# Paced loads in the first three steps, constants and the first plan on GpSimd, and a later first weight load, in an attention and mixture-of-experts kernel

## The chip, the cores and the metric

The kernel runs on one core of a Trainium2 chip. The metric is device microseconds of one execution; lower is better. The kernel before takes 458.71 us in the median of three runs (458.58 to 460.1).

## The reference, cut to what matters

```python
# q, k, v: (4, 8, 768, 64); every position sees 8 global keys and the 96 last ones
scores = q @ k.T / 8 - slope[h] * dist;  scores = where(keep, scores, -1e9)
x = softmax(scores) @ v                       # regrouped to rows: (3072, 512)
logits = x @ w_gate + modality_bias[modality_id]
e_idx, gate_w = argmax(logits), softmax(logits)[e_idx]        # 8 experts, top 1
for e in range(8):
    m = e_idx == e
    out[m] = gate_w[m] * (relu(x[m] @ w1[e]) @ w2[e])         # 512 -> 1024 -> 512
```

## The kernel before, in words

**Attention** goes over 24 blocks of 128 rows (6 to each of the 4 batches), in a software pipeline that is written out by hand in `step(n)` (L1054), for n from 0 to 24. Step n does the score matmuls of block n (`s_mm`, L210, 32 of them), adds the bias and takes the maximum of its 8 heads on VectorE (`red`, L229) and their exponentials on ScalarE (L240); it transposes the probabilities of block n-1 (`t_mm`, L254; copied back by `t_cp`, L263 on VectorE and L261 on ScalarE), does the value matmuls of block n-2 (`pv`, L276 with the tile `vl`, then L288 with `vx`) and scales them into rows (`xr`, L309) that go to the HBM tensor `x_rows` (L316). The gate's small matmuls run three and four steps behind (`gate_a`, `gate_b`, `gate_c`).

**Loads.** All come from the one queue of SyncE (SP), in the order of its program: `qt` and `kt` of block n+2 and `vx`, `vl` of block n are issued in step n, with three buffers each, so a load waits only for the matmuls that last read its buffer. At the start `load_0` and the loads of block 1 come first, then those of step 0 without any wait. Steps 3 to 10 also write zeros to the table of sorted tokens (`consts_c`, L974).

**Work set for a step.** `at(n, f)` adds work to the end of step n. For batch b the routing is `route_a` (maximum, exponential, one-hot), `route_b` (counts by matmul, running base on GpSimd), `route_d` (two sums, a reciprocal, the place of each token, all on VectorE) and `route_c` (a GpSimd scatter of token ids for each block), in steps 9, 10, 11 and from 12 on for batch 0, and six steps later for batch 1. `consts_b` (L939 to L946) and `consts_d` (L953 to L961) make constants on VectorE in steps 3 and 4.

**The plan of the first units.** After batch 1 is routed, `plan_e` works out on VectorE, in four parts in steps 17, 18, 18 and 19, which expert and which rows the first three full units of 256 tokens have (`items`, L418, and `slots`, L488). SP reads the result into registers (`ld_w` L588, `ld_x` L570) and then loads the first unit's weights: `w1` of the expert in quarters in steps 19 and 20 (L598, 512 KB each), `w2` in step 22 (L600). `split` (L609 on ScalarE, L610 on VectorE) makes high and low parts of one quarter at the end of each of the steps 21 to 24.

**The expert layers** (14 units, L638 to L640 and L679 to L681) then run with TensorE always busy. The order on TensorE, VectorE and ScalarE is fixed as written (`manual_schedule`); the order on SP and GpSimd is the scheduler's own. Three lines show where the change hooks in: a wait can be put on any instruction with `spaced`, and `last` always holds the newest ScalarE instruction.

```python
def spaced(ins, by=last):                       # L106: ins waits for by[0]
last[0] = nc.scalar.activation(...)             # L240, in red
at(LAST - 1 + (0, 1, 1, 2)[j], plan_e)          # L1018, LAST = 18
```

Of the kernel before, what the change touches and what calls it, by code (L numbers as in the profile page):

```python
# [12 lines left out]
I32 = mybir.dt.int32  # L13
# [25 lines left out]
NE = 3  # L39
BE = 2  # L40
# [30 lines left out]
def moe_attention_kernel(  # L71
# [56 lines left out]
    def load_k(n):  # L128

        kts[n] = qkn.tile([P, NP, KW], F32, tag="kt", name=f"kt{n}")  # L130
        nc.sync.dma_start(kts[n], k_t[n])

    def load_v(n):

        vx = qkn.tile([P, 2, DM], F32, tag="vx", name=f"vx{n}", bufs=3)
        vl = qkn.tile([P, 2, NP, D], F32, tag="vl", name=f"vl{n}", bufs=3)
        vxs[n] = vx, vl
        nc.sync.dma_start(vx, v_l[n])
        for h in range(2):
            nc.sync.dma_start(vl[64 * h : 64 * h + SM], v_s[n, h])  # L140
# [208 lines left out]

    def route_a(b):  # L350
# [5 lines left out]
        ex = t3(b, "ex")  # L356
        nc.scalar.activation(ex, dl, AF.Exp)
# [6 lines left out]
        rt[b] = oh  # L364
        rt[b, "ex"] = ex
# [25 lines left out]
    def route_d(b):  # L391
        se = t2(b, "se")
        V.reduce_sum(se, rt.pop((b, "ex")), axis=AX.X)
        V.tensor_scalar_add(se, se, 1e-9)
        V.reciprocal(tki.bitcast(F32)[:, b * NB : (b + 1) * NB, 1], se)
        pf = t2(b, "pf")
        V.reduce_sum(pf, rt.pop((b, "pos")), axis=AX.X)
        pi = t2(b, "pi", I32)
        V.tensor_copy(pi, pf)
# [18 lines left out]
    def items(tag, pool, cnt, used, ni, first):  # L418
# [6 lines left out]
        left = cnt  # L425
        if used is not None:
            left = pl("left", [E])
            V.scalar_tensor_tensor(left, used, -float(U), cnt, ALU.mult, ALU.add)
# [11 lines left out]
        if first:  # L440

            V.tensor_scalar(first_used, cex, -1.0, float(first), ALU.mult, ALU.add)
            V.tensor_scalar(first_used, first_used, 0.0, None, ALU.max)
            V.tensor_tensor(first_used, first_used, full, ALU.min)
# [11 lines left out]
        if not first:  # L456
            rem = pl("rem", [E])
            V.scalar_tensor_tensor(rem, full, -float(U), left, ALU.mult, ALU.add)
            key = pl("key", [E])
            V.scalar_tensor_tensor(key, rem, 8.0, erev, ALU.mult, ALU.add)  # L460
            V.tensor_tensor(t88, bm(key, E), bc(key, E), ALU.is_gt)
            rr = pl("rr", [E])
            V.reduce_sum(rr, t88, axis=AX.X)
            V.tensor_scalar(rr, rr, cin[:, E - 1 : E], None, ALU.add)
            V.tensor_scalar(key, rem, 0.0, 1000.0, ALU.is_equal, ALU.mult)
            V.tensor_add(rr, rr, key)
            yield
            V.tensor_tensor(m2, bm(rr, ni), uc, ALU.is_equal)
            V.tensor_add(m1, m1, m2)
            V.tensor_tensor(m2, m2, bm(full, ni), ALU.mult)  # L470
            V.tensor_add(st, st, m2)
            if used is not None:
                V.tensor_tensor(m2, m1, bm(used, ni), ALU.mult)
                V.tensor_add(st, st, m2)
            yield
# [416 lines left out]
    uidx = const.tile([P, NLT], F32, name="uidx")  # L892
    le = const.tile([P, E, E], F32, name="le")
# [13 lines left out]
    def consts_a():  # L907
# [5 lines left out]
        nc.gpsimd.iota(uidx, pattern=[[1, NLT]], base=0, **ciota)  # L913
        nc.gpsimd.memset(tki, 0)
# [19 lines left out]
    def consts_b():  # L934
# [4 lines left out]
        V.tensor_copy(m1, mi[:, :, 0])  # L939
        V.tensor_scalar(m0, m1, -1.0, 1.0, ALU.mult, ALU.add)  # L940
        V.tensor_tensor(gsame, bc(uidx[:, 0:NGT], NR), bm(uidx[:, 0:NR], NGT), ALU.is_equal)
        tb1 = gp.tile([P, NBLK, E], F32, tag="tb1", name="tb1", bufs=1)
        V.tensor_tensor(tbias, bc(m0, E), bm(mb[:, 0, :], NBLK), ALU.mult)
        V.tensor_tensor(tb1, bc(m1, E), bm(mb[:, 1, :], NBLK), ALU.mult)
        V.tensor_add(tbias, tbias, tb1)
        V.tensor_tensor(le, bm(eidx, E), bc(eidx, E), ALU.is_le)  # L946

    def consts_d():
# [28 lines left out]
    for b in range(B):  # L977
        n0 = b * NB
        at(n0 + NB + 3, route_a, b)
        at(n0 + NB + 4, route_b, b)  # L980
        at(n0 + NB + 5, route_d, b)
# [10 lines left out]
    early = {}  # L992

    def run(name, g, f=None):

        try:
            next(g)
        except StopIteration as r:
            f(r.value)
            return False  # L1000
        return True


# [3 lines left out]
    def planned_e(r):  # L1007
        uei, uoi, inv = slots("e", plan, *r, NE, 2)
# [3 lines left out]
    def plan_e(g=[]):  # L1012
        if not g:
# [40 lines left out]
    def step(n):  # L1054

        on, back = n < NBLK, 0 < n <= NBLK
        if on:
            load_v(n)
# [286 lines left out]
```

## Time and profile before

| what | value |
|---|---|
| median of the runs | 458.71 us |
| the profiled execution, its own time | 461.01 us |
| its span, first to last instruction | 459.2 us |
| TensorE busy | 439.6 us (96%) |
| VectorE / ScalarE / GpSimd busy | 323.7 / 283.5 / 100.9 us |
| mean granted TensorE clock | 0.991 |

Times are microseconds from the start of the span. A busy time is summed over an engine's instructions; `[2.37 <-DMA kt<-in_k_t]` behind an instruction is the idle time of its engine just before it and what ended it. SPq rows are issues of transfers. A step is read here by the start of its 32 score matmuls (L210).

### The profile page before, as it was taken

The numbers are of one execution on the slowest core, as the hardware profiler recorded it, in microseconds if no ns is written. First come the engines' busy times: TensorE is split into PE (matmuls) and PEld (weight loads), VectorE is DVE, ScalarE is ACT, GpSimd is POOL, SyncE is SP. The second block draws the span as 40 slices with busy tenths as digits, with TensorE's granted clock in tenths as the row PEclk, the third lists the DMA queues.
The fourth block names the chain that finished last, engine by engine and source line by source line (L and its number), as shares of the span: only waits on it lengthen the run. The fifth ranks groups of instructions, "written<-read, shape, count | busy, mean of one in ns | idle before, by whom it ended". The sixth has DMA issues, their size and how long they took to land.

```text
span 459.2 us, 12892 instructions
## 1 busy us (share of the span) xinstructions
PE 439.6 (96%) x4828; PEld 387.6 (84%) x4828; DVE 323.7 (70%) x973; ACT 283.5 (62%) x687; POOL 100.9 (22%) x144
## 2 busy tenths in 40 slices
PE   5799999998988999999999999999999999999994
PEld 5688888887877798989898988989889898899993
DVE  4789888889988669896656596574965648667450
ACT  5678887887777554554545486454854557655541
POOL 7000002123306341631312112213122040300101
PEclk9799999999999999999999999999999999999999
DMA  7999999999799919576757679666796666965101
GB/s 231 327 343 337 347 334 332 324 323 310 257 297 330 340 50 328 187 237 226 264 215 245 213 255 362 215 226 226 242 380 238 210 229 208 360 244 185 46 2 51
DMA packets 42870, 115.69 MB, mean 252 GB/s; under 512 B 8943, under 2 KB 10991, under 8 KB 42800
## 3 DMA queue, kind: packets, MB, share of 16 engines
q1 hardware_dynamic: 38032, 101.74, 66.4%
q0 software_dynamic: 4768, 13.05, 7.5%
q8 instruction: 40, 0.66, 0.6%
q14 instruction: 30, 0.25, 0.2%
HBM read 100.40 MB, written 14.63 MB: 250 GB/s over the span
## 4 chain that ended last, share of the span: by engine, by line
PE 81%; DVE 7%; issue 6%; DMA 3%; ACT 2%; SPq 0%; POOL 0%; POOLq 0%; DVEq 0%; ACTq 0%
PE pt L254 7%; PE phs L638 6%; PE phs L640 6%; PE phs L639 6%; PE pos L681 6%; PE pos L680 6%; PE pos L679 6%; PE s L210 5%; PE x L288 4%; PE phe L638 2%; PE poe L679 2%; PE poe L681 2%; PE poe L680 2%; PE phe L640 2%; PE phe L639 2%
## 5 line engine op out<-in xcount | busy, mean ns | idle before, releaser
L240 ACT ACTIVATE pr<-sc,nmx 128x168 f32<-128x168 f32 x192 | 81.2, 425 | 26.1 <-DVE nmx L229 26.1
L640 PE MATMUL phs<-xhs,als 128*128 128x256 f32 x256 | 72.3, 282 | 0.0
L638 PE MATMUL phs<-xhs,ahs 128*128 128x256 f32 x256 | 72.2, 282 | 0.0
L639 PE MATMUL phs<-xls,ahs 128*128 128x256 f32 x256 | 72.1, 282 | 0.0
L645 DVE SCALAR_TENSOR_TENSOR hls<-phs,hhs 128x512 fp32r<-128x512 f32 x32 | 22.1, 692 | 51.8 <-ACT hhs L644 51.8
L229 DVE CUSTOM_DVE_ANT_0 sc<-s,tbl 128x168 f32<-128x168 f32 x192 | 50.7, 329 | 10.9 <-PE s L210 9.9
L254 PE MATMUL pt<-ident,pr 128*128 128x128 f32 x288 | 46.3, 292 | 5.4 <-DVE pT L263 3.0
L679 PE MATMUL pos<-bhs,hhs 128*128 128x512 f32 x128 | 51.4, 401 | 0.0
L681 PE MATMUL pos<-bhs,hls 128*128 128x512 f32 x128 | 50.6, 395 | 0.0
L680 PE MATMUL pos<-bls,hhs 128*128 128x512 f32 x128 | 50.5, 395 | 0.0
L644 ACT ACTIVATE hhs<-phs 128x512 fp32r<-128x512 f32 x32 | 19.1, 598 | 48.9 <-PE phs L640 48.9
L638 PEld LDWEIGHTS phs<-xhs,ahs 128*128 128x128 f32 x256 | 48.9, 191 | 0.4
L639 PEld LDWEIGHTS phs<-xls,ahs 128*128 128x128 f32 x256 | 48.8, 191 | 0.3
L640 PEld LDWEIGHTS phs<-xhs,als 128*128 128x128 f32 x256 | 48.8, 191 | 0.0
L577 POOL DMA_INDIRECT xgs<-x_rows,uis x16 | 20.9, 1304 | 126.6 <-DMA uis<-ids_sorted 63.8
L254 PEld LDWEIGHTS pt<-ident,pr 128*128 128x128 f32 x288 | 31.2, 144 | 17.8 <-DVE pT L263 8.9
L263 DVE COPY pT<-pt 128x384 f32<-128x384 f32 x72 | 37.2, 545 | 6.9 <-PE pt L254 6.8
L210 PE MATMUL s<-kt,qt 64*64 64x168 f32 x768 | 36.6, 321 | 3.9 <-DMA kt<-in_k_t 3.9
L405 POOL DMA_INDIRECT ids_sorted<-tki,pi x24 | 25.3, 1055 | 62.5 <-PE x L288 28.4
L240 ACT ACTIVATION_READ_ACCUMULATOR pr<-sc,nmx 128x1 f32 x192 | 36.3, 189 | 0.0
L210 PEld LDWEIGHTS s<-kt,qt 64*64 64x64 f32 x768 | 27.5, 138 | 6.9 <-issue 5.0
L697 POOL DMA_INDIRECT out<-obs,ois x16 | 17.4, 1089 | 54.2 <-ACT obs L696 52.0
(322 smaller groups left out, 1054.8 us busy)
## 6 DMA issues: line engine op xcount, KB each, us to landing
vx<-in_v_l SPq DMA_DIRECT2D x24, 512.0 KB, 6.5
kt<-in_k_t SPq DMA_DIRECT2D x23, 464.0 KB, 6.7
x_rows<-xr SPq DMA_DIRECT2D x24, 256.0 KB, 5.5
qt<-in_q_t SPq DMA_DIRECT2D x23, 256.0 KB, 5.3
vl<-in_v_s SPq DMA_DIRECT2D x48, 96.0 KB, 5.7
rawe0a<-in_moe_w SPq DMA_DIRECT2D x4, 512.0 KB, 4.9
rawe0b<-in_w SPq DMA_DIRECT2D x4, 512.0 KB, 6.5
rawe1a<-in_moe_w SPq DMA_DIRECT2D x4, 512.0 KB, 3.7
```

Of the source, the lines that this page charges most:

```text
L210: nc.tensor.matmul(ps[h][64 * half : 64 * half + 64, c : c + W], qt[hs, hp, 64 * half : 64 * half + 64], kt[hs, hp, k0 : k0 + W], start=Tr ...
L229: V.tensor_tensor_reduce(out=sc, in0=pss[n, hp // 2][h][:, hp % 2 * W : (hp % 2 + 1) * W], in1=(tbl0 if n % NB == 0 else tbl)[:, hh, :], o ...
L240: last[0] = nc.scalar.activation(pr[:, h * (PRW - W) : h * (PRW - W) + W], sc, AF.Exp, bias=nmx[:, hh : hh + 1], scale=-1.0, accum_out=sum ...
L254: nc.tensor.transpose(tp[:, j * P : (j + 1) * P], pr[:, o : o + P], ident)
L263: V.tensor_copy(pT.rearrange("p a b -> p (a b)"), tp[:, 0 : 3 * P])
L405: ins = nc.gpsimd.indirect_dma_start(out=ids, out_offset=bass.IndirectOffsetOnAxis(ap=pi[:, j : j + 1], axis=0), in_=tki[:, b * NB + j, :] ...
L638: nc.tensor.matmul(o, hi[:, fs], s.xh[:, c, :], start=(c == 0), stop=False)
L639: nc.tensor.matmul(o, hi[:, fs], s.xl[:, c, :], start=False, stop=False)
L640: nc.tensor.matmul(o, lo[:, fs], s.xh[:, c, :], start=False, stop=(c == 3))
L679: nc.tensor.matmul(s.po[t], s.hh[:, fc, tt], hi[:, wv], start=(fc == 0), stop=False)
L680: nc.tensor.matmul(s.po[t], s.hh[:, fc, tt], lo[:, wv], start=False, stop=False)
L681: nc.tensor.matmul(s.po[t], s.hl[:, fc, tt], hi[:, wv], start=False, stop=(fc == 7))
```

## The change

**The start.** A new `paced` puts a wait on the newest ScalarE instruction of the program before a load, for `qt` and `kt` of blocks 2 to 4 and for `vx` and `vl` of blocks 0 to 2. In steps 0 to 2 the loads of `qt` and `kt` are issued behind the first six heads of `red`, so they wait for the sixth exponential of the step; the value loads of block n-1 are issued at the start of step n (for n from 1 to 3) and wait for the last ScalarE instruction of step n-1. **GpSimd.** `consts_b`, `consts_d`, all of `plan_e` (one piece in step 17) and the two sums of `route_d` for batches 0 to 2 go to GpSimd; a sum over eight becomes three adds of halves (`folded`), a comparison a subtraction and a comparison with zero (`over`). The exponential of `route_a` becomes `route_e`, one step later. **Weights.** The quarters of the first unit's `w1` are loaded in steps 20 and 22, its `w2` in step 24.

```diff
+    def paced(ins, early):
+        if early:
+            spaced(ins)
     def load_q(n):
-        nc.sync.dma_start(qts[n], q_t[n])
+        paced(nc.sync.dma_start(qts[n], q_t[n]), 1 < n < NPACE + 2)     # NPACE = 3
     def load_v(n):
-        nc.sync.dma_start(vx, v_l[n])
+        paced(nc.sync.dma_start(vx, v_l[n]), n < NPACE)
...
+    def folded(r, t):
+        G = nc.gpsimd
+        h = E // 2
+        while h > 1:
+            G.tensor_add(t[:, :, 0:h], t[:, :, 0:h], t[:, :, h : 2 * h])
+            h //= 2
+        G.tensor_add(r.unsqueeze(2), t[:, :, 0:1], t[:, :, 1:2])
+    def over(r, a, b, op):
+        nc.gpsimd.tensor_tensor(r, a, b, ALU.subtract)
+        nc.gpsimd.tensor_scalar(r, r, 0.0, None, op)
...
+    def route_e(b):
+        ex = t3(b, "ex")
+        nc.scalar.activation(ex, rt.pop((b, "dl")), AF.Exp)
-    def route_d(b):
+    def route_d(b, eng):
         se = t2(b, "se")
-        V.reduce_sum(se, rt.pop((b, "ex")), axis=AX.X)
-        V.tensor_scalar_add(se, se, 1e-9)
+        pf = t2(b, "pf")
+        for r, t in ((se, rt.pop((b, "ex"))), (pf, rt.pop((b, "pos")))):
+            if eng is V:
+                V.reduce_sum(r, t, axis=AX.X)
+            else:
+                folded(r, t)
+        eng.tensor_scalar(se, se, 1e-9, None, ALU.add)
         V.reciprocal(tki.bitcast(F32)[:, b * NB : (b + 1) * NB, 1], se)
...
-        V.tensor_copy(m1, mi[:, :, 0])              # consts_b, consts_d: V -> nc.gpsimd
+        nc.gpsimd.tensor_copy(m1, mi[:, :, 0])
...
-    for j in range(4):
-        at(LAST - 1 + (0, 1, 1, 2)[j], plan_e)
+    at(LAST - 1, plan_e)                            # its sums by folded, on GpSimd
...
-    at(LAST + 1, lambda: ld_w(eslots[0], "a", (0, 1)))
-    at(LAST + 2, lambda: ld_w(eslots[0], "a", (2, 3)))
+    at(LAST + 2, lambda: ld_w(eslots[0], "a", (0, 1)))
+    at(LAST + 4, lambda: ld_w(eslots[0], "a", (2, 3)))
-    at(LAST + 4, lambda: ld_w(eslots[0], "b"))
+    at(LAST + 6, lambda: ld_w(eslots[0], "b"))
...
     def step(n):
-        if on:
+        if 0 < n <= NPACE:
+            load_v(n - 1)
+        if NPACE <= n < NBLK:
             load_v(n)
-        if n + 2 < NBLK:
+        if NPACE <= n < NBLK - 2:
             load_q(n + 2)
             load_k(n + 2)
...                                                 # behind red of six heads:
+        if n < NPACE:
+            load_q(n + 2)
+            load_k(n + 2)
```

**The order on SP at the start**, before, from the load of block 1 on (`qt1` is the tile qt of block 1):

```order
L118 DMA qt1_82<-in_q_t 128x512
L131 DMA kt1_84<-in_k_t 128x928
L138 DMA vx0_225<-in_v_l 128x1024
L140 DMA vl0_226<-in_v_s 48x512 x2
L118 DMA qt2_230<-in_q_t 128x512
L131 DMA kt2_232<-in_k_t 128x928
L138 DMA vx1_280<-in_v_l 128x1024
L140 DMA vl1_281<-in_v_s 48x512 x2
L928 DMA cst_182<-in_small 128x196
L118 DMA qt3_285<-in_q_t 128x512
L131 DMA kt3_287<-in_k_t 128x928
L138 DMA vx2_374<-in_v_l 128x1024
```

and of the change, from the wait for the sixth exponential of step 0 (on `qt2`) to the value loads of block 2:

```order
L124 DMA qt2_266<-in_q_t 128x512
L137 DMA kt2_268<-in_k_t 128x928
L144 DMA vx0_276<-in_v_l 128x1024
L146 DMA vl0_277<-in_v_s 48x512 x2
L124 DMA qt3_322<-in_q_t 128x512
L137 DMA kt3_324<-in_k_t 128x928
...
L124 DMA qt4_416<-in_q_t 128x512
L137 DMA kt4_418<-in_k_t 128x928
L124 DMA qt5_501<-in_q_t 128x512
L137 DMA kt5_503<-in_k_t 128x928
L322 DMA x_rows<-xr0_475 128x512
L144 DMA vx2_491<-in_v_l 128x1024
```

The value loads of block 0 have moved behind `qt`, `kt` of block 2, and those of block 2 behind `qt`, `kt` of blocks 4 and 5 and the first write of rows.

**The order on VectorE at the end of step 17**, before, from the last gate addition to the first reduction of step 18 (the nine L430 to L444 are the first part of the plan):

```order
L342 TENSOR_TENSOR lgt_2486<-lq_1_2641,tbias 128x8
L393 TENSOR_REDUCE se_2645<-ex_2344 128x6
L394 TENSOR_SCALAR se_2645<-se_2645 128x6
L395 RECIPROCAL tki<-se_2645 128x6
L397 TENSOR_REDUCE pf_2649<-pos_2503 128x6
L399 CAST pi_2651<-pf_2649 128x6
L430 CAST cie<-base 128x8
...
L444 TENSOR_TENSOR first_used<-first_used,fulle 128x8
L229 ISA sc_0_2698,nmx_2697<-s_0_0_2676,tbl_130 128x168
```

and of the change:

```order
L269 COPY pT_2_2643<-pt_2_2639 128x384
L348 TENSOR_TENSOR lgt_2494<-lq_1_2651,tbias 128x8
L423 RECIPROCAL tki<-se_2655 128x6
L235 ISA sc_0_2760,nmx_2759<-s_0_0_2738,tbl_130 128x168
L235 ISA nmx_2759 128x1
```

Thirteen of the fourteen instructions between the gate addition and the next block's first reduction are gone; the reciprocal stays.

**The order on SP behind the plan.** Before, the registers are read (`ueie`: the unit's expert, `uoie`: its rows) behind the value loads of block 20 and the rows of block 17. Of the change, from the value load of block 19:

```order
L144 DMA vx19_2868<-in_v_l 128x1024
L605 TENSOR_LOAD ueie_2696
...
L615 DMA rawe0a0_3171<-in_moe_w1 128x1024
L615 ISA
L615 DMA rawe0a1_3173<-in_moe_w1 128x1024
L587 TENSOR_LOAD uoie_2709
...
L322 DMA x_rows<-xr16_2840 128x512
...
L124 DMA qt22_3028<-in_q_t 128x512
L137 DMA kt22_3030<-in_k_t 128x928
L146 DMA vl20_3024<-in_v_s 48x512 x2
L144 DMA vx20_3023<-in_v_l 128x1024
```

SP now waits for the plan with the loads of block 22, the value loads of block 20 and the rows of block 16 queued behind the wait.

## Rows read from the trace of the kernel before

**Rows 1.** Windows of the span: in each stretch its length, busy time and instructions of each engine, granted clock, DMA share, GB/s.

```profile
0.00:10.19 10.19, 5.21 (x73) 4.55 (x73) 5.21 (x33) 6.72 (x25) 8.77 (x40) 1.00 0.76 223
10.19:40.22 30.03, 26.80 (x509) 22.81 (x509) 24.49 (x133) 20.36 (x89) 0.00 (x0) 0.89 1.03 332
...
101.48:120.94 19.46, 17.27 (x369) 14.78 (x366) 17.55 (x99) 13.44 (x58) 6.99 (x15) 1.00 0.87 280
...
155.63:433.50 277.87, 277.68 (x1754) 247.75 (x1754) 184.92 (x289) 158.51 (x206) 62.62 (x53) 1.00 0.68 236
```

**Rows 2.** TensorE in order of time, 7 to 46 us: start, duration, what, and the idle time before it.

```profile
7.01 0.80 PE L210 MATMUL s<-kt,qt 64*64 64x168 f32 x16 [1.57 <-DMA kt<-in_k_t]
10.19 2.43 PE L210 MATMUL s<-kt,qt 64*64 64x168 f32 x32 [2.37 <-DMA kt<-in_k_t]
15.22 1.37 PE L210 MATMUL s<-kt,qt 64*64 64x168 f32 x32
16.41 0.65 PE L276 MATMUL x<-vl,pT 40*64 40x64 f32 x32
...
21.27 1.44 PE L254 MATMUL pt<-ident,pr 128*128 128x128 f32 x6 [2.32 <-DVE xr L309]
22.64 2.12 PE L210 MATMUL s<-kt,qt 64*64 64x168 f32 x32
28.37 1.37 PE L210 MATMUL s<-kt,qt 64*64 64x168 f32 x32
34.43 1.39 PE L210 MATMUL s<-kt,qt 64*64 64x168 f32 x32
40.22 1.39 PE L210 MATMUL s<-kt,qt 64*64 64x168 f32 x32
45.70 1.39 PE L210 MATMUL s<-kt,qt 64*64 64x168 f32 x32
```

**Rows 3.** Transfers issued in the first 42 us: count, KB of each, median us from issue to landing.

```profile
kt<-in_k_t SPq DMA_DIRECT2D x8, 464.0 KB, 6.0
vx<-in_v_l SPq DMA_DIRECT2D x7, 512.0 KB, 8.0
qt<-in_q_t SPq DMA_DIRECT2D x2, 128.0 KB, 2.3
```

**Rows 4.** ScalarE, the sixth and the eighth exponential of step 0.

```profile
8.76 0.42 ACT L240 ACTIVATE pr<-sc,nmx 128x168 f32<-128x168 f32 x1
9.59 0.42 ACT L240 ACTIVATE pr<-sc,nmx 128x168 f32<-128x168 f32 x1
```

**Rows 5.** Two windows of the start (columns as in rows 1), and of 18.4 to 20 us the queue that brings instructions: packets, MB, share.

```profile
10.00:15.00 5.00, 4.57 (x43) 3.64 (x44) 3.35 (x19) 3.31 (x17) 0.00 (x0) 0.66 1.04 306
20.00:25.00 5.00, 3.73 (x68) 3.23 (x69) 1.72 (x10) 0.93 (x5) 0.00 (x0) 0.66 1.06 330
...
q8 instruction: 1, 0.02, 5.2%
```

**Rows 6.** VectorE alone in four stretches: length, busy time and instructions, clock, DMA. They are the first part of the plan with `route_d`, its second part, `consts_b` and `consts_d` (each with the edge of a neighbour).

```profile
107.85:110.65 2.80, 2.42 (x17) 1.00 0.89 299
115.06:117.05 1.99, 1.75 (x14) 1.00 0.47 174
28.85:30.56 1.71, 1.64 (x9) 1.00 1.03 298
34.86:36.30 1.44, 1.27 (x12) 1.00 1.04 315
```

**Rows 7.** TensorE, the score matmuls of steps 17 to 21 (30 of the 32 of step 17; the last two have a row of their own).

```profile
101.48 1.70 PE L210 MATMUL s<-kt,qt 64*64 64x168 f32 x30
...
107.42 1.39 PE L210 MATMUL s<-kt,qt 64*64 64x168 f32 x32
...
114.62 1.39 PE L210 MATMUL s<-kt,qt 64*64 64x168 f32 x32
...
120.94 1.39 PE L210 MATMUL s<-kt,qt 64*64 64x168 f32 x32
126.42 1.39 PE L210 MATMUL s<-kt,qt 64*64 64x168 f32 x32
```

**Rows 8.** GpSimd: the running bases of batches 1 and 2 (six dependent adds each) and a scatter; then all adds of that line (min/median/max ns).

```profile
102.21 1.60 POOL L382 TENSOR_TENSOR base<-base,pks 128x8 f32<-128x8 f32 x6 [2.25 <-DVE pks L379]
...
105.16 1.03 POOL L405 DMA_INDIRECT ids_sorted<-tki,pi  x1 [0.36 <-PE x L288]
...
141.32 2.50 POOL L382 TENSOR_TENSOR base<-base,pks 128x8 f32<-128x8 f32 x6
...
L382 POOL TENSOR_TENSOR base<-base,pks x18: 200/202/1096, 68.6 to 143.6; 128x8 f32<-128x8 f32 x18
```

**Rows 9.** The four loads of the first weights on SP, the reading of its registers (min/median/max ns), and the landing of one `qt` load issued at 108.88 us.

```profile
122.58 2.97 SPq L598 DMA_DIRECT2D rawe0a<-in_moe_w  x4
...
L588 SPq TENSOR_LOAD <-ueie x3: 266/266/467, 121.6 to 131.1; - x3
...
qt<-in_q_t SPq DMA_DIRECT2D x1, 256.0 KB, 4.0
```

**Rows 10.** ScalarE and VectorE around the splits at the ends of steps 21 and 22.

```profile
132.97 0.25 ACT L357 ACTIVATE ex<-dl 128x48 f32<-128x48 f32 x1 [0.54 <-DVE dl L355]
141.13 1.22 DVE L610 TENSOR_TENSOR ale<-rawe0a,ahe 128x1024 fp32r<-128x1024 f32 x1 [1.13 <-ACT ahe L609]
```

More of the change, by code (lines that the diff above doesn't have):

```diff
@@ L39 @@
 NE = 3
+NU = 8
+NPACE = 3
 BE = 2
@@ L415, in route_c, with items @@
         scat.append(ins)
-    def items(tag, pool, cnt, used, ni, first):
+    def items(tag, pool, cnt, used, ni):
         def pl(name, shape, dt=F32):
             return pool.tile([P] + shape, dt, name=f"{name}{tag}")
[L425 to L428, printed above, removed]
+        left = pl("left", [E])
+        V.scalar_tensor_tensor(left, used, -float(U), cnt, ALU.mult, ALU.add)
         ci = pl("ci", [E], I32)
@@ L439, in items @@
         V.tensor_sub(cex, cin, full)
[L440 to L444, printed above, removed]
         yield
@@ L455, in items @@
         yield
[L456 to L475, printed above, removed]
+        rem = pl("rem", [E])
+        V.scalar_tensor_tensor(rem, full, -float(U), left, ALU.mult, ALU.add)
+        key = pl("key", [E])
+        V.scalar_tensor_tensor(key, rem, 8.0, erev, ALU.mult, ALU.add)
+        V.tensor_tensor(t88, bm(key, E), bc(key, E), ALU.is_gt)
+        rr = pl("rr", [E])
+        V.reduce_sum(rr, t88, axis=AX.X)
+        V.tensor_scalar(rr, rr, cin[:, E - 1 : E], None, ALU.add)
+        V.tensor_scalar(key, rem, 0.0, 1000.0, ALU.is_equal, ALU.mult)
+        V.tensor_add(rr, rr, key)
+        yield
+        V.tensor_tensor(m2, bm(rr, ni), uc, ALU.is_equal)
+        V.tensor_add(m1, m1, m2)
+        V.tensor_tensor(m2, m2, bm(full, ni), ALU.mult)
+        V.tensor_add(st, st, m2)
+        V.tensor_tensor(m2, m1, bm(used, ni), ALU.mult)
+        V.tensor_add(st, st, m2)
+        yield
         ust = pl("ust", [ni])
@@ L913, in consts_a @@
         nc.gpsimd.iota(uidx, pattern=[[1, NLT]], base=0, **ciota)
+        nc.gpsimd.iota(ufull, pattern=[[U, NU]], base=U, **ciota)
         nc.gpsimd.memset(tki, 0)
@@ L978, in moe_attention_kernel @@
         n0 = b * NB
+        eng = nc.gpsimd if b + 1 < B else V
         at(n0 + NB + 3, route_a, b)
+        at(n0 + NB + 4, route_e, b)
         at(n0 + NB + 4, route_b, b)
-        at(n0 + NB + 5, route_d, b)
+        at(n0 + NB + 5, route_d, b, eng)
         for j in range(NB):
@@ L1009, in planned_e @@
         for u in range(NE):
             eslots.append(mk(f"e{u}", uei[0:1, u : u + 1], uoi[0:1, u : u + 1], inv[:, :, u], xd[0 : BE * S, :], 2))
-    def plan_e(g=[]):
-        if not g:
-            g.append(items("e", plan, base[:, BE - 1, NB, :], None, NE, NE))
-        run("e", g[0], planned_e)
-    for j in range(4):
-        at(LAST - 1 + (0, 1, 1, 2)[j], plan_e)
+    at(LAST - 1, plan_e)
     def open_moe():
@@ L1131, in rest @@
                     yield
-        r = yield from items("b", plan, base[:, B - 1, NB, :], first_used, NI, 0)
+        r = yield from items("b", plan, base[:, B - 1, NB, :], first_used, NI)
         uei, uoi, inv = slots("b", plan, *[t[:, 0:NS] for t in r], NS, 2)
```

102 lines of the change are left out of this document (70 added, 32 removed).

## The prediction

> **What bounds the kernel now.** I read the windows by stage first [rows 1]. From 155.63 to 433.5 us TensorE is busy 277.68 of 277.87 us: the expert layers run at its pace, so a step that starts earlier in the attention part ends the kernel earlier by as much. Before that there are two stretches with gaps. From 10.19 to 40.22 us TensorE is busy 26.80 of 30.03 us, with the transfers at 332 GB/s and a share of 1.03; from 101.48 to 120.94 us it is busy 17.27 of 19.46 us.
>
> Second, the timeline of TensorE, read as the starts of the score matmuls [rows 2]. A step that nothing disturbs takes 5.48 us (40.22 to 45.70). Steps 4 and 5 take 6.06 and 5.79. Before them there are other losses: step 1 begins 2.37 us late for its `kt`, and in step 2 TensorE sits idle for 2.32 us, from 18.95 to 21.27; behind that the score matmuls of step 3 take 2.12 instead of 1.39 us, because the granted clock stands at 1.2 instead of 2.4 GHz for a time (a mean of 0.66 from 20 to 25 us, [rows 5]). In the middle stretch steps 17, 18 and 19 take 5.94, 7.20 and 6.32 us [rows 7].
>
> Third, what VectorE does in those steps: 2.80 and 1.99 us of plan and routing sums stand behind steps 17 and 18, and `consts_b`, `consts_d` (1.71 and 1.44 us) behind steps 3 and 4 [rows 6]. In the hand-written order the next block's reductions wait behind them, and TensorE behind those.
>
> **The change part by part.** The sum is made on the profiled execution (span 459.2 us, its own time 461.01), which is 2.3 us above the median of the runs, 458.71; I take the gains off the median.
>
> *Constants off VectorE.* All of `consts_b` and `consts_d` leaves it. Steps 4 and 5 should fall to the undisturbed period: 0.58 + 0.31 = **0.89 us**. GpSimd has nothing to do between 10.19 and 40.22 us [rows 1], so its some 20 small instructions there hide in that gap; their first user is the gate addition of step 4, which begins at 28.37 us.
>
> *Routing and plan off VectorE.* Of the 2.80 us behind step 17 the reciprocal stays (0.2 us, one of fourteen instructions). Step 18 falls from 7.20 to the period, 1.72 us; step 19 from 6.32, 0.84 us: **2.56 us**. Step 17 keeps its 5.94, since counting matmul and copy stay. The third part of the plan, behind step 19, was already covered: step 20 takes 5.48. `route_d` of batches 0 and 2 stood beside other waits; I cost it at nothing.
>
> *The exponential of `route_a`.* At the end of step 21 ScalarE waits 0.54 us for VectorE before it, with the split queued behind [rows 10]. Moved a step on it needs no wait, but now stands ahead of the next split, for which VectorE already waits 1.13 us: 0.5 less 0.2, **0.3 us**.
>
> *Weights later.* The first split is at the end of step 21, the third at the end of step 23. Quarters 0 and 1 keep at least a step, quarters 2 and 3 about one; with some 6 us to land [rows 3] this is hidden: 0. If a quarter came late, VectorE's split and the reductions behind it would be late by the same time.
>
> *SP behind the plan.* This is the wait that the change adds. On GpSimd, 51 small instructions and one scatter stand between the counts of batch 1 (used first 0.73 us into step 17, [rows 7, 8]) and the cast of `ueie`. Six dependent adds take 1.60 us, 0.267 each [rows 8]; the scatter with its gap 1.4: the result is there 0.73 + 13.6 + 1.4 = 15.7 us after the start of step 17. SP stands still behind the value loads of block 19, with the rows of block 16, `qt`/`kt` of block 22 and the value loads of block 20 behind it. After the result it reads registers (0.27 to 0.47 us each), issues two quarters and more register reads: `kt` of block 22 follows about 5.5 us later, and lands in 4 us (a near-empty queue, [rows 9]). That is 25.2 us after the start of step 17; step 22 begins at 5.94 + 4 x 5.48 = 27.9. So the wait is covered by 2.7 us: **0**. The cover is gone from 0.32 us for an instruction on (2.7 / 51 more).
>
> *The start.* Nothing in the trace shows loads held back, so I bound it. Upper end: step 1 begins when step 0's matmuls end (7.81 instead of 10.19 us), TensorE never stops before 21.27, and step 4 begins 4.0 us earlier (2.4 at step 1, the rest from the stop and its half clock, less what ScalarE and VectorE need). Lower end: held loads land late. `qt`, `kt` of block 2 go out at 9.2 us, with the sixth exponential, `vx` and `vl` of block 0 at 10.1, with the eighth [rows 4]. With the medians of 6.0 and 8.0 us [rows 3] they land at 15.6 and 18.1; the value matmuls of block 0 began at 16.41 [rows 2], so everything is 1.7 us late: **-1.7**. Between them I count bytes, since the queue is full from then on. Up to the value loads of block 2 there are 6 x 720 + 3 x 704 + 256 + 98 KB = 6.79 MB. 1.54 MB of it is moved before the hold, and the flow starts again at about 11.2 us (9.2, and 2 us to the first data, as 128 KB took 2.3 us); the other 5.25 MB at 332 GB/s [rows 1] take 15.8 us, and landing 1.8: 28.8 us. The value matmuls of block 2 began 1.2 us into step 4, at 29.6. So step 4 can come at most 0.8 us earlier, whatever was won ahead of it: I take **0.5 us**, near the middle row, as the flow at that time is the bound.
>
> The sum is 0.89 + 2.56 + 0.3 + 0 + 0.5 = 4.25 us: 459.2 goes to about 455, and the median to **454.5 us**, if nothing of it is given back; the transition at 140 to 156 us keeps the same work.
>
> **The rivals.**
>
> *GpSimd is late and SP with it (slower).* The same six adds took 2.50 us, 0.417 each, where VectorE ran a large subtraction of two SBUF operands, and the longest add 1.096 us [rows 8]. At 0.417 the plan is ready 51 x 0.15 = 7.6 us later, 4.9 us beyond the cover; the stop would halve the clock as at 20.8 us, some 1.2 us more (2.12 against 1.39, 1.44 against 1.01, [rows 2]). 458.71 - 4.25 + 6.1 = 460.6 us. Against it: in steps 17 to 20 no such subtraction runs, and the base of batch 1 kept 0.267 beside the reductions. The point at which it begins is 0.32 us an instruction, and slower than before from 0.38 on. The Trainium skill (GPSIMD Engine Reference, 4.1 Engine selection) sends adds and sums along the free axis to VectorE, with GpSimd about twice as slow for two inputs. By that, from VectorE's 0.2 us an instruction, an estimate of 0.4 us would lie in this rival; the row of 0.267 speaks against it, so it keeps a small chance.
>
> *The start is won whole.* If the transfers are not the bound and the stop in step 2 goes, the start gives 4.0 instead of 0.5: 451.0 us. For it: at the stop a packet of 0.02 MB of instructions is under way in the full queue [rows 5], so lighter traffic could bring it earlier. Against it: the count of bytes. The Trainium skill (Runtime: NRT & Kernel Launch, Instruction fetch mechanics) holds that refills are mostly hidden; by that the stop would have another cause and would stay.
>
> *The hold costs the start.* Loads land with the medians of the full queue: -1.7 instead of 0.5, 456.7 us. For it: the rate was 306 GB/s from 10 to 15 us [rows 5], and the queue would idle some 2.5 us.
>
> *The hold does nothing.* If the kernel's first `kt` lands as before, the start changes only by the constants: 455 us; this lies in the forecast's own range.
>
> **How the numbers follow.** Forecast 454.5 us, own range 453 to 456: 0.58. Start won whole, 451: 0.13. Hold costs, 456.7: 0.17. GpSimd late, 460.6: 0.12. A measurement tells 0.3% (1.4 us) from no change, so faster is below 457.3 and slower above 460.1. Faster: 0.57 + 0.13 + 0.10 = 0.80; same: 0.01 + 0.06 + 0.04 = 0.11; slower: 0.01 + 0.08 = 0.09. The range from 450.7 to 458.2 leaves out about half of the whole start (0.07) and most of the late plan (0.11).
>
> **What would show it.** Right: score matmuls of steps 18 and 19 at 5.5 us, of steps 4 and 5 too; SP issuing `kt` of block 22 about 21 us after the start of step 17 and TensorE not waiting for it; step 4 beginning between 27 and 28.5 us, with its wait, if any, at the value matmuls of block 2. Wrong: TensorE waiting for a `kt` in step 22; small GpSimd instructions above 0.32 us; the start of step 4 past 29 us or before 26; gaps in steps 18 or 19 that another releaser holds.

## The result and the profile after

The changed kernel takes 462.24 us in the median of 17 runs, the kernel before 459.1 in as many beside it: a ratio of 1.0065, 95% interval 1.0037 to 1.0092. It is slower; the forecast was 454.5 us. Runs more than 1.5% above a kernel's fastest are left out of every ratio here. The profiled execution took 462.44 us (span 460.7).

The windows by stage of the changed kernel, cut at the same times as [rows 1], with the same columns:

```profile
0.00:10.19 10.19, 7.83 (x108) 6.84 (x109) 6.34 (x40) 6.71 (x26) 9.07 (x42) 1.00 0.51 155
10.19:40.22 30.03, 23.05 (x478) 19.29 (x480) 21.80 (x111) 20.93 (x91) 5.12 (x20) 1.00 0.96 323
40.22:101.48 61.26, 60.21 (x1327) 52.34 (x1325) 50.89 (x272) 48.46 (x201) 7.81 (x23) 1.00 1.00 333
101.48:120.94 19.46, 19.46 (x408) 17.20 (x408) 16.52 (x81) 16.47 (x69) 15.69 (x64) 1.00 0.93 307
120.94:155.63 34.69, 30.51 (x630) 26.39 (x624) 26.98 (x116) 24.26 (x86) 16.47 (x31) 0.95 0.95 324
155.63:433.50 277.87, 277.73 (x1772) 247.36 (x1768) 186.78 (x293) 159.67 (x208) 62.62 (x53) 1.00 0.69 236
```

The fourth line is what the change was written for: TensorE has no gap there, against 2.2 us of gaps before. The second line goes the other way, 23.05 us busy instead of 26.80. The place is seen in TensorE's order of time (start, duration, what, idle time before), the answer to [rows 2]:

```profile
8.34 1.48 PE L216 MATMUL s<-kt,qt 64*64 64x168 f32 x32 [1.02 <-DVE nmx L235]
...
14.86 1.37 PE L216 MATMUL s<-kt,qt 64*64 64x168 f32 x32 [1.56 <-DMA kt<-in_k_t]
17.04 0.96 PE L282 MATMUL x<-vl,pT 40*64 40x64 f32 x32 [0.81 <-DMA vl<-in_v_s]
...
21.15 1.37 PE L216 MATMUL s<-kt,qt 64*64 64x168 f32 x32
...
26.14 1.37 PE L216 MATMUL s<-kt,qt 64*64 64x168 f32 x32
30.03 0.93 PE L282 MATMUL x<-vl,pT 40*64 40x64 f32 x32 [2.52 <-DMA vl<-in_v_s]
...
34.59 1.39 PE L216 MATMUL s<-kt,qt 64*64 64x168 f32 x32
```

Steps 1 to 4 begin 1.85, 0.4, 1.5 and 2.2 us earlier than in [rows 2]; then TensorE waits 2.52 us for the value loads of block 2, and step 5 begins at 34.59 instead of 34.43 us. All that was won, the constants' part included, is given back in one wait. Windows of 2 us show why (columns as above; the second to last number is the DMA share):

```profile
6.00:8.00 2.00, 1.01 (x24) 0.52 (x16) 1.64 (x13) 1.58 (x8) 2.00 (x4) 1.00 0.68 253
8.00:10.00 2.00, 1.66 (x34) 1.46 (x35) 1.25 (x11) 2.00 (x11) 1.86 (x4) 1.00 0.01 2
10.00:12.00 2.00, 0.63 (x6) 0.39 (x4) 1.82 (x13) 2.00 (x11) 1.93 (x8) 1.00 0.64 165
...
18.00:20.00 2.00, 1.89 (x38) 1.58 (x38) 0.61 (x2) 1.64 (x8) 0.00 (x0) 1.00 0.77 263
20.00:22.00 2.00, 1.79 (x30) 1.47 (x34) 1.75 (x5) 0.48 (x1) 0.00 (x0) 1.00 0.73 201
```

From 8 to 10 us the transfers stand still at 2 GB/s: the loads that could run are held, and those in flight have landed. From 18 to 22 us the share is low a second time: SP issues nothing from 15.3 to 18.8 us, where `qt` of block 4 waits for the sixth exponential of step 2.

The routing and the plan, the answer to [rows 7] and [rows 8]: TensorE's score matmuls of steps 17 to 21, then GpSimd's cast of the plan, then SP's issue of `kt` of block 22, one fence for each engine.

```profile
103.74 1.49 PE L216 MATMUL s<-kt,qt 64*64 64x168 f32 x32
109.33 1.39 PE L216 MATMUL s<-kt,qt 64*64 64x168 f32 x32
114.81 1.39 PE L216 MATMUL s<-kt,qt 64*64 64x168 f32 x32
120.29 1.39 PE L216 MATMUL s<-kt,qt 64*64 64x168 f32 x32
125.77 1.39 PE L216 MATMUL s<-kt,qt 64*64 64x168 f32 x32
```

```profile
115.00 0.19 POOL L361 TENSOR_TENSOR uexpe<-uexpe 128x6 f32<-128x6 f32 x1
...
115.92 0.18 POOL L1049 CAST ueie<-uexe 128x3 int32<-128x3 f32 x1
```

```profile
123.38 1.10 SPq L137 DMA_DIRECT2D kt<-in_k_t  x1
```

Steps 18 to 21 take 5.48 us each. The plan is there 12.4 us after the start of step 17, and `kt` of block 22 is issued 19.6 us after it; nobody waits for it.

The end of the attention part, TensorE in order of time:

```profile
142.93 0.60 PE L329 MATMUL tx<-ident,xr 128*128 128x128 f32 x4
...
146.24 0.89 PE L282 MATMUL x<-vl,pT 40*64 40x64 f32 x32 [1.02 <-DMA vl<-in_v_s]
147.80 1.19 PE L294 MATMUL x<-vx,pT 128*64 128x64 f32 x32 [0.67 <-DMA vx<-in_v_l]
...
150.84 1.06 PE L329 MATMUL tx<-ident,xr 128*128 128x128 f32 x4
...
157.50 0.36 PE L655 MATMUL phe<-xhe,ahe 128*128 128x256 f32 x1
```

In step 24 TensorE waits for the value loads of block 22, which SP now issues (at 136.9 us) behind 2 MB of the first unit's weights. Behind the waits the four transposes of L329 take 1.06 us, a step earlier 0.60: the granted clock is 1.2 GHz for a time (a mean of 0.95 in the fifth window above). From step 22 to the first matmul of the experts it is 26.25 us, before 23.72.

### The profile page after: what moved, and what is told of

Read it like the earlier page. It is cut to its first block, busy times and chain, and to the rows that moved or that the text cites. A ratio compares the mean times of both kernels' runs of the same rounds, so it can differ in the third digit from the quotient of the medians.

```text
span 460.7 us, 12930 instructions
## 1 busy us (share of the span) xinstructions
PE 440.3 (96%) x4828; PEld 388.5 (84%) x4828; DVE 317.0 (69%) x918; ACT 284.0 (62%) x687; POOL 120.2 (26%) x232
## 4 chain that ended last, share of the span: by engine, by line
PE 84%; DMA 6%; issue 5%; DVE 2%; ACT 2%; SPq 0%; POOL 0%; POOLq 0%; ACTq 0%
PE pt L260 7%; PE phs L655 6%; PE phs L657 6%; PE phs L656 6%; PE pos L698 6%; PE pos L697 6%; PE pos L696 6%; PE s L216 5%; PE x L294 5%; DMA vl<-in_v_s 3%; PE x L282 3%; PE phe L655 3%; PE phe L657 2%; PE phe L656 2%; PE poe L696 2%
## 5 line engine op out<-in xcount | busy, mean ns | idle before, releaser
L594 POOL DMA_INDIRECT xgs<-x_rows,uis x16 | 24.0, 1500 | 110.8 <-DMA uis<-ids_sorted 63.9
L216 PE MATMUL s<-kt,qt 64*64 64x168 f32 x768 | 35.0, 310 | 3.2 <-DMA kt<-in_k_t 1.9
L216 PEld LDWEIGHTS s<-kt,qt 64*64 64x64 f32 x768 | 26.4, 132 | 5.8 <-DMA kt<-in_k_t 1.8
```

The costliest lines, as they stand in the source:

```text
L216: nc.tensor.matmul(ps[h][64 * half : 64 * half + 64, c : c + W], qt[hs, hp, 64 * half : 64 * half + 64], kt[hs, hp, k0 : k0 + W], start=Tr ...
```

## The experiments

A ratio is that of a kernel's times to those of the kernel before beside it. The kernel before took 459 to 460 us in three of the six comparisons and 464 in the other three (the result is the first of the six), so kernels are compared through their ratios, and best within one comparison. Steps are named by the start of their score matmuls.

### First comparison: which part costs

Each kernel is the change with parts undone, or one part alone.

```diff
 e1_gp_weights:  -NPACE = 3              +NPACE = 0      (no hold, loads at their old places)
 e2_hold_gp:     weights back: at(LAST+1, w1 0,1) at(LAST+2, w1 2,3) at(LAST+4, w2)
 e3_gp_only:     both of these
 e4_hold_only:   the kernel before + paced(...) and the new order of the loads in step(n)
```

> The changed kernel without the hold: every load stands where it stood before; the moves to GpSimd and the later weights stay. Theory (three separate losses: the hold gives nothing at the start and brings TensorE's late instruction packets in steps 7 to 17, the weights cost the transition): step 7 begins at about 44.8 us (45.70 less 0.89), steps 7 to 17 take 55.8 us as before, steps 17 to 22 gain 2.6, and from step 22 to the first expert matmul it takes some 26 us (26.25 in the change, 23.72 before): about 458, ratio 0.997. Rival (the gaps of steps 7 to 17 are chance, or come with the GpSimd work): steps 7 to 17 take 58 us here too, ratio 1.002.

Measured: 0.9978 (0.9946 to 1.0010). Step 5 begins at 28.70 us. Steps 7 to 17 take 58.93 us without any hold, which is the rival's sign.

> The changed kernel with the first unit's weights back in steps 19, 20 and 22; hold and GpSimd moves stay. Theory (the weights' place cost the transition 2.5 us): from the start of step 22 to the first expert matmul 23.7 us again, value loads of block 22 waited for by nobody; the start and steps 7 to 17 as in the change (58.2 us): ratio 1.001. Rival (the transition is late because GpSimd's scatters are, and with them the token lists): still some 26 us, ratio 1.006.

Measured: 1.0003 (0.9970 to 1.0036). TensorE waits 0.9 us for `vl` of block 0 and 1.6 for that of block 2 (0.8 and 2.5 in the change). From step 22 to the experts it is 24.58 us, between the two.

> Only the moves to GpSimd and of the exponential; loads and weights stand as before. Theory: 0.89 + 2.56 + 0.3 us stay won and nothing is lost: 455.4 us, ratio 0.992. Rival (GpSimd's work delays the token lists, or shifts TensorE's instruction packets): ratio 0.998 or above, with steps 7 to 17 over 57 us or the transition over 25.

Measured: 0.9952 (0.9917 to 0.9987), between the two. Step 5 at 30.89 us.

> The kernel before with only the hold on the loads of the first three steps. Theory (the hold gives nothing at the start, and brings late instruction packets to steps 7 to 17): step 7 at about 46.5 us, steps 7 to 17 some 58.2 us, 462.2 us, ratio 1.007. Rival (the hold costs nothing, the gaps were chance): step 7 at 45.7, steps 7 to 17 55.8 us, ratio 1.000.

Measured: 1.0078 (1.0048 to 1.0109). Step 5 at 33.92 us, with a `vl` wait of 1.3 us; steps 7 to 17 take 56.76 us, between the two.

What follows: by the times the hold alone is worth the whole loss (some 3.6 us), and the GpSimd moves alone are a gain, smaller than the 3.75 us forecast for them. Of the 3.6 us the trace of e4 shows 0.9 at step 5 (33.0 us in the mean of three traces of the kernel before, taken in other comparisons). Half of my theory falls: late packets in steps 7 to 17 do not need the hold (e1), and without it the start is won by 3.5 to 5.7 us against [rows 2], or 2.1 to 4.3 against that mean, not by the constants' 0.89.

### Second comparison: TensorE's stops at packet ends

The traces show stops of TensorE that no engine or load ends ("issue"), as in step 9 of the changed kernel:

```profile
56.52 1.36 PE L216 MATMUL s<-kt,qt 64*64 64x168 f32 x29
58.17 0.36 PE L216 MATMUL s<-kt,qt 64*64 64x168 f32 x2 [0.29 <-issue]
```

Counting TensorE's instructions in the trace, the stop is at number 1984, which is 192 more than a multiple of 256. Each transfer of the queue that brings its instructions is 16 KB, one for 256 instructions. I thought that the hold brought these stops to steps 7 to 17.

```diff
 e5_before_again, e6_change_again:  unchanged
 e7_before_no_mid_loads, in load_q, load_k, load_v of the kernel before
   (e8_hold_no_mid_loads: the same in e4):
+    if n in range(8, 17):
+        qts[n] = qts[n - 1];  return          # kts, vxs alike
```

> The kernel before, unchanged, for a trace from the same chip as the runs beside it. If TensorE's stops at the ends of its 256-instruction packets belong to the changed kernel, there are none here between 40 and 155 us; if they come and go with the state of the queue, there are one to four of them here too.

Measured: three such stops, at 33.49, 39.77 and 63.63 us, each at 192 or 193 of 256; 460.54 us. Step 5 at 31.93 us.

> The changed kernel, unchanged, for a second trace of it. Theory (the hold gives the start nothing, and stops at the ends of instruction packets cost steps 7 to 17 some 2.4 us): step 7 begins 0 to 1 us before that of the kernel before, steps 7 to 17 take over 57 us. Rival (the stops were chance): under 56.5 us.

Measured: 459.27 us; steps 7 to 17 take 56.85 us, between the two. Step 5 at 34.34 us.

> The kernel before with the loads of blocks 8 to 16 left out (their steps use the buffers of block 7). Theory (TensorE's stops without a releaser are late instruction packets in a full queue): steps 8 to 15 at 5.48 us each, every packet begins within 1 us of the end of the one before it, no such stop; some 0 to 1 us faster than before. Rival (they have another cause): stops remain at the places 192 of each 256 instructions.

Measured: 1.0737. Another routing follows from the other data, and the expert part is 34 us longer, so only the attention part is read. Steps 8, 9 and 12 to 15 take 5.48 us, steps 10 and 11 5.70 and 5.93, all with no stop.

> The hold alone on the kernel before, and the loads of blocks 8 to 16 left out. Theory (the hold's cost of 3.6 us arises in steps 7 to 17 from late instruction packets): with an idle queue there the hold costs under 1.5 us against the same kernel without the hold. Rival (the cost arises at the start, in the held loads): it still costs 3 us or more.

Measured: 1.0826, so the hold costs 3.6 us here too (497.28 against 493.69).

What follows: the theory of e8 falls. The hold's cost does not need the loads of steps 7 to 17; it is there when these are gone. That it arises at the start, as the rival has it, these two traces do not show: they differ by 1.35 us as a whole, 0.75 at step 5 and 1.1 in steps 7 to 17 (the experts give some back). Nor do the stops belong to the hold: over all 20 traces of this study there are 32 of them from 18 to 105 us, each at 192 or 193 of 256, in kernels with and without the hold, the kernel before among them. What they are can be read from the packets; times in us, worked out from the trace's packet records:

```
kernel                 end of   packet begins after   TensorE goes on     from end
                       packet   the end before it     after it landed     to end
changed kernel          58.2            3.7                 1.3             6.3
changed kernel          99.7            2.7                 1.4             6.2
e12_gp_again            69.0            5.0                 1.4             7.3
e7, no loads there      74.2            0.1                 4.0             5.7
e7, no loads there      90.9            0.4                 3.6             5.6
kernel before, step 2   21.3            7.5                 1.4            10.2
changed kernel, step 2  20.2            6.2                 3.7            11.2
```

In these rows a packet begins, at the earliest, when TensorE enters the one before it. In an empty queue it is there 4 us early. In a full one it begins 2.7 to 5.0 us late, takes 0.9 to 2.1 us, and TensorE goes on 1.3 to 1.4 us after it has landed: when that comes to more than the 5.6 us in which it works off a packet, TensorE stops.

The last two rows settle the stop of 2.32 us in step 2 of [rows 2], which the row puts down to VectorE: it stands at such a place too (number 448), and TensorE went on 1.4 us after the packet had landed. All three traces of the kernel before stop there (2.32, 1.28 and 0.94 us), and so do e7 (2.77), e12 (2.92) and e18 (1.98). In the change and in e1, e3, e11, e15 and e16 the packet is there 3 us or more before it is used. So much of what the start wins beyond the constants is this packet (step 2 takes 5.0 to 6.3 us in these five, 6.9 to 7.4 in the kernel before); whether the moves to GpSimd bring it earlier, or chance does, is not shown.

### Third comparison: which part of the hold

The base is e3 (GpSimd moves, weights at their old steps).

```diff
 e9_hold_values:  only vx, vl of blocks 0 to 2 a step later and paced
 e10_hold_qk:     only qt, kt of blocks 2 to 4 behind the sixth reduction and paced
 e11_order_only:  the loads at the change's places in step(n), and in paced(): -spaced(ins)  +pass
 e12_gp_again:    e3 itself
```

> The GpSimd moves with half of the hold: the value loads of blocks 0 to 2 are issued a step later and wait for ScalarE; `qt`, `kt` stand as before. Theory (the hold costs the queue time that it leaves idle, and the value loads of block 2, last in the queue, are what TensorE then waits for): little queue time is idle, but the value loads are still the last; TensorE waits under 2 us for `vl`, step 5 begins at 30 to 32 us, ratio 0.996 to 1.000. Rival (it is the loads of `qt`, `kt` that may not be late): as without the hold, 0.995, and the other half costs all.

Measured: 0.9948 (0.9915 to 0.9980); 0.16 us of waiting for `vl` (of block 0), step 5 at 31.52 us, as the theory had it; the ratio is the rival's. This run has the value loads of block 2 nearly where the change has them, behind `qt`, `kt` of blocks 4 and 5 and the first rows. The issue of their `vx` on SP in the change, here, and in e15 below, in this order:

```profile
22.37 0.38 SPq L144 DMA_DIRECT2D vx<-in_v_l  x1
...
21.24 0.33 SPq L144 DMA_DIRECT2D vx<-in_v_l  x1
...
13.24 0.37 SPq L143 DMA_DIRECT2D vx<-in_v_l  x1
```

What differs at the start is that `qt`, `kt` are not held, so the queue does not stand still. The value matmuls of block 2, in step 4, begin 3.0 us earlier than in the change (27.01 against 30.03), with no wait to speak of:

```profile
6.00:8.00 2.00, 1.40 (x28) 0.77 (x20) 1.24 (x9) 1.18 (x7) 2.00 (x4) 1.00 1.00 373
8.00:10.00 2.00, 0.44 (x7) 0.47 (x11) 0.96 (x8) 2.00 (x11) 1.86 (x4) 0.92 1.04 374
10.00:12.00 2.00, 2.00 (x31) 1.65 (x23) 0.94 (x7) 1.16 (x7) 1.91 (x8) 0.50 1.01 315
```

```profile
25.56 1.37 PE L216 MATMUL s<-kt,qt 64*64 64x168 f32 x32
27.01 0.88 PE L282 MATMUL x<-vl,pT 40*64 40x64 f32 x32
```

> The GpSimd moves with the other half: `qt`, `kt` of blocks 2 to 4 are issued behind the sixth maximum and wait for ScalarE; the value loads stand as before, and so go ahead of them. Theory: `qt`, `kt` of block 2 go out at some 9.4 us behind 2.1 MB of values, land at about 15.5 us, and step 2 begins 1.5 to 2 us late; nobody waits for `vl`; ratio 0.998 to 1.002. Rival (these loads cost all of it): as with the whole hold, 1.000 to 1.003, step 5 at 34 us or later.

Measured: 1.0065 (1.0034 to 1.0096). `kt` of block 2 comes 3 us later than I expected:

```profile
9.38 1.48 PE L216 MATMUL s<-kt,qt 64*64 64x168 f32 x32 [2.23 <-DMA kt<-in_k_t]
18.41 2.52 PE L216 MATMUL s<-kt,qt 64*64 64x168 f32 x32 [4.41 <-DMA kt<-in_k_t]
```

Here the queue is full (share 0.98 from 5 to 10 us), and the order is bad: what is needed first stands behind three blocks of values. It is another mechanism than the change's, at the same price.

> The GpSimd moves with the loads in the order of the change (`qt`, `kt` of two blocks ahead, values a step later), but with no wait for ScalarE. Theory (idle queue time is the cost): no wait for `vl`, step 5 at 29 to 31 us, ratio 0.995, as without the hold. Rival (the order is the cost: the value loads stand last whatever holds them): TensorE waits for `vl` of block 2, step 5 after 33 us, ratio 1.000.

Measured: 0.9936 (0.9904 to 0.9969); no `vl` wait, step 5 at 30.46 us. But this run does not have the order of the change: the order on SP is the scheduler's own, and without the wait it puts the value loads of block 2 (issued from 13.5 us) ahead of `qt`, `kt` of blocks 4 and 5 (from 15.8), where the change issues them behind these, at 22.4 us. So it does not test the rival. e9 comes nearer, with the late place and a queue that runs: there the place costs next to nothing.

> The moves to GpSimd alone once more, for the same chip as the three beside it, with a second trace. Theory (with every load at its old place, the start is won by some 3 us and TensorE waits for no `vl`): step 5 before 32 us, steps 17 to 22 in 27.5 to 28 us, as in the change, unless the stops without a releaser on the earlier chip (30.9 us) belong to the kernel; ratio 0.992 to 0.996.

Measured: 0.9966 (0.9929 to 1.0002). Step 5 at 32.63 us, so the bound of 32 was missed: there is a stop of 2.9 us at a packet's end at 19.87 us. Steps 17 to 22 take 31.82 us, with the stops of the fifth comparison.

### Fourth comparison: the wait, and the weights, side by side

```diff
 e13_change:            the changed kernel
 e14_hold_old_weights:  e2 (weights in steps 19, 20, 22)
 e15_no_wait:           the change with, in paced():  -spaced(ins)  +pass
 e16_order_again:       e11 (e15 with the weights in steps 19, 20, 22)
```

> The changed kernel once more, as the measure of the three beside it. Ratio 1.004 to 1.009 as before; if the stops without a releaser at 116 to 124 us belong to the chip, they may be here too.

Measured: 1.0090 (1.0048 to 1.0132).

> The change with the first unit's weights back in steps 19, 20 and 22. Theory (the later weights put the value loads of block 22 behind them, and TensorE waits for these in step 24): 0.3 to 0.6% faster than the change beside it. Rival (the weights' place costs nothing, and the difference between the earlier two runs was the chip's): within 0.2% of it.

Measured: 1.0074 (1.0035 to 1.0114), 0.16% below the change: the rival's side.

> The change without the wait for ScalarE: the order of the loads, the GpSimd moves and the later weights stay. Theory (the wait leaves the queue idle from about 5 to 11 us, and that is lost): 0.7 to 1.0% faster than the change beside it, no wait for `vl` of block 2, step 5 before 32 us. Rival (the order and the weights cost it): under 0.3% faster.

Measured: 0.9985 (0.9948 to 1.0021), 1.05% or 4.9 us below the change (3.5 us between the two medians, 466.94 and 463.41). Taking the wait away, and nothing else in the program, turns the loss into none; on SP the value loads of block 2 move to 13.2 us with it, as in e11. Its windows of 2 us and TensorE's rows, against those of the changed kernel above:

```profile
6.00:8.00 2.00, 0.80 (x16) 0.52 (x16) 1.90 (x15) 2.00 (x10) 2.00 (x4) 1.00 0.96 331
8.00:10.00 2.00, 0.79 (x22) 0.82 (x26) 0.13 (x2) 1.94 (x10) 1.86 (x4) 1.00 0.99 331
10.00:12.00 2.00, 1.50 (x24) 1.02 (x16) 1.82 (x15) 1.45 (x7) 1.43 (x4) 1.00 1.05 357
```

```profile
9.21 1.49 PE L215 MATMUL s<-kt,qt 64*64 64x168 f32 x32 [2.31 <-DMA kt<-in_k_t]
13.75 1.37 PE L215 MATMUL s<-kt,qt 64*64 64x168 f32 x32
...
25.91 0.65 PE L281 MATMUL x<-vl,pT 40*64 40x64 f32 x32
...
30.19 1.45 PE L215 MATMUL s<-kt,qt 64*64 64x168 f32 x30
```

The queue never stands still; the lost share of the three windows adds up to 3.3 us (0.28 + 0.98 + 0.41, times 2 us). The value matmuls of block 2 begin 4.1 us earlier, without a wait, and step 5 by 4.4 us; against the trace of e13, beside it, by 2.3 and 2.7 us (28.21 and 32.88 there).

> The GpSimd moves with the loads in the order of the change, no wait for ScalarE, and the weights at their old steps: the candidate that beats both. Ratio to the kernel before 0.990 to 0.997; if the later weights cost something without the wait too, it is 0.2 to 0.5% faster than the kernel beside it that has them.

Measured: 0.9973 (0.9935 to 1.0012), 0.12% below e15; both bounds were missed by little. Between e14 and e16 the wait is worth 1.01%. The later weights cost 0.26% (e1 against e3), 0.16% and 0.12%, each inside its interval, all of one sign.

### Fifth comparison: the stops of steps 18 to 22, and the best version

In the first, third and fourth comparison the kernels with the GpSimd moves show stops between 110 and 125 us that are at no packet's end. TensorE in e13, the changed kernel itself:

```profile
118.19 0.55 PE L260 MATMUL pt<-ident,pr 128*128 128x128 f32 x3 [0.81 <-issue]
118.79 1.39 PE L216 MATMUL s<-kt,qt 64*64 64x168 f32 x32
121.04 0.30 PE L282 MATMUL x<-vl,pT 40*64 40x64 f32 x2 [0.38 <-issue]
121.76 0.56 PE L282 MATMUL x<-vl,pT 40*64 40x64 f32 x16 [0.42 <-issue]
```

There steps 17 to 22 take 31.28 us, where the same program took 27.51 in the trace above.

> The kernel before, for a third trace. If the chip is one of the slower ones and the stops belong to it, steps 17 to 22 take over 30.8 us and there are stops away from the packet ends here too; if they belong to the GpSimd moves, 30.4 us and no such stop.

Measured: 459.40 us on the same chip as the fourth comparison, with no such stop (one at a packet's end, at 62.51 us); steps 17 to 22 take 30.41 us, step 5 is at 32.63. The kernel before is back at 459.83 us here.

> The GpSimd moves, the loads in the order of the change without the wait, the weights at their old steps, for a third interval. Ratio 0.992 to 0.998; steps 17 to 22 in 27.5 to 28 us on a chip without these stops (then 0.990 to 0.994), some 31 us on one with them.

Measured: 0.9898 (0.9864 to 0.9932), 455.98 us against 459.83: by the ratios it beats both kernels. Steps 17 to 22 take 28.36 us, with none of these stops (the traced execution took 459.92 us).

What follows: the same program and the same chip are met with and without these stops, in comparisons whose kernel before stands at 464 and at 460 us. They are a condition of the hour, not of the chip alone. What causes them, and whether the moves make a program more open to them, stays open: no trace of the kernel before was taken in such an hour. The nearest, e4 without the moves, took 30.92 us for steps 17 to 22 and has such stops only from 142 us on, which speaks for the moves making it so. Most of the stops of steps 18 to 22 stand near the same three places of the program (TensorE's instructions 4640, 4745 and 4765; each trace has the first two or the third).

## Why the prediction was wrong

The sum failed at one step, **the start**, and by little at a second, the later weights.

*The start.* I costed it at +0.5 us, with the byte count as the bound. The count came out 1.2 us too early: value loads of block 2 at 28.8 us, and their matmuls began at 30.03. It took the queue as full from 11.2 us on, and from 18 to 22 us it was not (0.77 and 0.73). That alone is more than the term. The step that failed above all is the comparison: "The value matmuls of block 2 began 1.2 us into step 4, at 29.6", so the flow at that time must be the bound with or without the hold. It was not. No trace without the wait has TensorE waiting for `vl` at all, and with the constants gone and the queue left running the matmuls begin at 25.91 (e15). Their old time was set by TensorE's own late start, the late packet of step 2 among it. So the idle queue time, 2.5 us as I had counted and 3.3 in the trace, was not hidden behind anything. Step 5 begins, in the mean of the traces:

```
GpSimd moves, with the wait (changed kernel, e6, e13, e14)                  34.5 us
kernel before (its first trace, e5, e17)                                    33.0
GpSimd moves, without the wait (e1, e3, e11, e12, e15, e16)                 30.2
```

The hold costs 4.3 us there; the times say 4.9 (e13 against e15). These are means of few traces: side by side it is 2.7 us (e13 against e15) and 7.7 (e14 against e16), and the ranges just keep apart, 32.88 to 36.35 with the wait and 28.61 to 32.63 without. (Two more traces lie within them: e2, with the wait, 35.58, and e18, without, 32.18.) Against the kernel before step 5 is 1.5 us late, where constants and start together were to bring 1.4. That the first trace of before had the latest step 5 of its three (34.43, 31.93, 32.63) hid this from me. So the start measures -2.1 us where I had +0.5: of the 7.2 us between my gain of 4.25 and the loss of 3.0 that the times show, 2.6. Of my signs, step 5 took 5.48 us as forecast, but step 4 8.46, with the wait in it.

*The rivals.* "The hold costs the start" had the mechanism, an idle queue, and its price of 1.7 us is near what step 5 shows against the kernel before (2.1 us by the means, with the constants' 0.58 taken out). Its time of 456.7 us was too low for what it left out, the transition and what no stage shows (below). "The start is won whole" had its condition half met: in the change the stop of step 2 went (0.32 us are left at that place, and the packet is there in time), but the bytes were the bound all the same. Without the wait step 4 begins at 24.5 us in the mean of the six traces, 3.9 us earlier than in [rows 2] and 2.5 than in the mean of three traces of before. "GpSimd is late" did not happen: the 52 small instructions came 0.20 us apart, not 0.267, and the cover was larger than forecast.

*Routing and plan.* Right in mechanism and nearly in size: steps 18 and 19 fell to 5.48, and steps 17 to 22 take 27.51 instead of 30.43 us, 2.9 against a forecast of 2.56 (step 17 gave 0.35 more). In the hours of the stops this gain is lost (31.28).

*Constants.* Step 4 takes 5.47 us in e16 instead of 6.05 in e17: 0.58, as forecast. In the changed kernel the `vl` wait covers it.

*Weights.* "This is hidden: 0" was wrong by a small term. The splits were in time, as I had costed, but I did not ask what stands behind the loads on SP: the value loads of block 22. From step 22 to the experts it is 26.25 and 23.86 us in two traces of the change, 23.70 to 23.76 before. Side by side the later weights cost 1.2 (e13 against e14), 1.3 (e15 against e16) and 0.4 us (e1 against e3) there; the times give 0.5 to 1.2 us, not resolved by any one comparison. That "the transition at 140 to 156 us keeps the same work" was the sentence that failed.

*The exponential.* Its 0.3 us was not measured by itself.

*What the sum leaves.* In the means of the two traces of the change without those stops (this one and e6) against the three of the kernel before, the stages come to -1.5 (start), -0.6 (steps 5 to 17), +2.7 (17 to 22) and -1.3 us (transition): 0.7 us slower, where the times say 3.0 (1.7 to 4.2). The two executions had a mean granted clock of 0.995 and 0.996; over the runs of the result it is 0.988, and there the time rises by 0.24 us for each 0.001 of clock less, some 1.7 us for this difference. That TensorE's waits leave a half clock behind them in most executions would fit: the mean clock over the runs is 0.982 to 0.991 in the kernels that hold `qt`, `kt` (the change, e2, e4, e10, e13, e14) and 0.989 to 0.995 in e1, e3, e9, e11, e12, e15, e16 and e18. It is not shown, as only the traced executions can be read; what is left, 0.6 us, is inside the interval.

## What to carry to other kernels

Before a load is held back, ask whether its queue will have anything else to move: a full queue that stands still for 3 us has lost 3 us of flow, and the load that is last in the order pays. When a wait is taken out to see what it cost, look whether the order of the loads has moved with it. A time at which work "began before" bounds nothing by itself; a wait row must show that it was the data that it waited for. And one trace is one execution: where a stage differs by 2 us between executions, as the start here, take several before a term of 0.5 us is read from it.

## What the runs showed of the hardware

- TensorE's instructions come in 16 KB packets through the DMA engines, one asked for as the one before is entered. With idle transfers a packet began 0.1 to 0.4 us after the last ended and was 3.6 to 4.0 us early; with full ones it began up to 8.0 us later, and stops of up to 2.9 us followed (both in e12, step 2). The Trainium skill (Runtime: NRT & Kernel Launch, Instruction fetch mechanics) holds that refills are mostly hidden; in the full queue here some nine in ten were (32 stops from 18 to 105 us in 20 traces, with some 15 packets in each).
- Small GpSimd instructions of two inputs took 0.18 to 0.24 us with 3 to 32 elements to a partition and 0.27 to 0.31 with 48 and 64 (the change, steps 17 to 19); most of VectorE's, in the kernel before, took 0.15 to 0.18 with 8 and 24 and 0.20 to 0.23 with 48 and 64. The Trainium skill (GPSIMD Engine Reference, 4.1 Engine selection) puts them at about twice VectorE's time; these rows show 1.2 to 1.5 times.
- Stops of TensorE at no packet's end, 0.2 to 1.0 us each, in whole comparisons at a time, with the kernel before at 464 instead of 460 us. Their cause is not known.
